# Attention decode, forward and backward: the spared DMA engine's rows dealt to other pairs of engines in each of five stores

## The chip, the cores and the metric

The kernel runs on 1 core of one Trainium2 chip. The metric is the device time of that core in microseconds (us), lower is better. Before the change it was 1276.73 us, the median of 3 runs (1276.36 to 1278.41).

## What is computed

64 heads (2 batches of 32), one query row each, 8192 keys and values of 128 numbers, all in bf16. The reference gives the attention output and the gradients of q, k and v:

```python
def _fwd_reference(q, k, v):
    scale = q.shape[-1] ** -0.5
    scores = jnp.einsum("bhqd,bhkd->bhqk", q, k) * scale
    p = _softmax(scores, axis=-1)
    return jnp.einsum("bhqk,bhkd->bhqd", p, v)

_out, _vjp = jax.vjp(_f, q, k, v)      # outputs: _out and the three gradients
_grads = _vjp(grad_out)
```

With one query row, the gradients of v and k are outer products: dV is the softmax weights times the row of grad_out, dK is the score gradient times the row of q. So 2 x 64 tensors of 2 MB are read (K and V of each head) and 2 x 64 of 2 MB are written (dK and dV). Nothing else that crosses to memory is large.

## The kernel before, in words

**Tiles.** K and V of one head each lie in a tile of 128 partitions (`kt`, `vt`), 64 tokens of 128 numbers on a partition, which is one contiguous row of 16 KB in memory. There are 5 such pairs of tiles (`UNITS`). SyncE's queue (SP) loads them with one transfer of 128 rows each (`load`, issued from L106).

**One head's work.** TensorE turns the tile in 64 steps (L115), ScalarE copies the results out of PSUM (L122, two of them in a head by VectorE, L120), TensorE forms the scores and the products with grad_out (L131), small steps form the softmax (L148 to L244), and TensorE sums the weighted rows (L256). VectorE then writes the outer products into the very tiles from which K and V were read (`outer`, L288: dV over `vt`, dK over `kt`), and the tiles are stored. The main loop interleaves the front half of head h with the back half of head h-1, in an order written out by hand.

**Stores.** `store(h, w, ...)` (w = 0 for dV, 1 for dK) issues one transfer of 128 rows of 16 KB from ScalarE's queue (L348). As ScalarE's instructions run in order, the issue of a store also stands ahead of the copies of L122 behind it. The last head is stored in halves.

**Five stores by pieces.** For one store in 26 (`RARE`; 2h + w = 12, 38, 64, 90, 116, always a dV) `store_by_fifteen` takes over and issues from GpSimd's queue (POOL). It sends the 128 rows in 24 transfers: for each r of 0 to 3 transfers of 11, 4, 2, 3, 8 and 4 rows (L316). The 16 DMA engines that move everything are called 0 to 15 here. A transfer of n rows from this queue puts its rows on n neighbouring engines, the next one goes on where it ended, and a tiny transfer `turn(n)` (L302: n rows of 2 x 4 bytes from q into the scratch tile `spare`) moves the starting place on by n without moving data that matters. The transfers of 4 rows are sent in pieces of 16 KB and not of 8 KB; they start at engine 0 and leave the starting place where it is. The packets of the trace bear this reading out: four engines have forty 16 KB packets of this queue each, one engine has no data packet of it. In this way the rows are laid so that the fifth engine (number 4) gets none: engine 0 to 3 and 5 to 15 get 8 rows each in a store, which is 120, and the 8 rows that engine 4 would have had (partitions 16 to 19 and 48 to 51) go in four transfers of 2 rows to four pairs of neighbouring engines. Those four transfers are `fifth(r)` before the change.

**What orders these transfers.** GpSimd runs its instructions in order. Eight semaphores are used in turn for the transfers of its queue, so each transfer waits for the landing of the one eight before it. After a store by pieces the tile it left is next loaded ten heads later (V of head 16 is the first load that waits for GpSimd's transfers), because the pool gives out tiles in the order in which they come free.

Of the kernel before, what the change touches and what calls it, by code (L numbers as in the profile page):

```python
# [16 lines left out]
QG = 4  # L17
OG = 4
RARE = 26
UNITS = 5  # L20


@with_exitstack
def kernel(
# [41 lines left out]

    kvp = ctx.enter_context(tc.tile_pool(name="kv", bufs=UNITS))
    evp = ctx.enter_context(tc.tile_pool(name="ev", bufs=5))
# [29 lines left out]
    def load(h):  # L98
        x = heads[h]
        x.ev = {}  # L100
        x.kv = [
            kvp.tile([P, NT, D], BF16, name="kt", tag="kt"),
            kvp.tile([P, NT, D], BF16, name="vt", tag="vt"),
        ]
        for dst, src in zip(x.kv, (k_v, v_v)):
            nc.sync.dma_start(out=dst[:], in_=src[h])  # L106
# [108 lines left out]
    def weights_v(h):  # L215
        x = heads[h]
        x.rl, x.rls = rl_all[:, 0, h : h + 1], rl_all[:, 1, h : h + 1]
        to_weights(0, x.E)
        nc.vector.reciprocal(out=x.rl, in_=x.lsum)
        x.w2 = [doubled("P2", x.E, x.rl)]  # L220
        nc.vector.tensor_scalar(
            out=x.rls, in0=x.rl, scalar1=scale, scalar2=None, op0=ALU.mult
        )
# [73 lines left out]
    def turn(n):  # L297

        i = 4 * len(turns)
        turns.append(n)  # L300
        two = lambda t: t.rearrange("p (a b) -> p a b", a=2)
        nc.gpsimd.dma_start(  # L302
            out=two(spare[0:n, :])[:, :, i : i + 2], in_=two(q_rows[0:n, :])[:, :, 0:2]
        )

    def store_by_fifteen(h, w):

        dst, src = (dv_v, dk_v)[w][h], heads[h].kv[1 - w]

        def rows(lo, n, step=4, size=8192):
            own = slice(lo, lo + step * (n - 1) + 1, step)
            nc.gpsimd.dma_start(out=dst[own], in_=src[own], max_dma_last_dim=size)  # L316

        def fifth(r):
            rows(16 + r, 2, step=32)

        for r in range(4):

            if r == 1:
                fifth(r)
                turn(14)
            rows(52 + r, 11)
            rows(r, 4, size=16384)
            if r == 0:
                fifth(r)
                turn(3)  # L330
            elif r == 3:
                turn(10)
                fifth(r)
                turn(9)
            else:
                turn(5)
            rows(20 + r, 3)
            if r == 2:
                fifth(r)
                turn(14)  # L340
            rows(96 + r, 8)
            rows(32 + r, 4, size=16384)
            turn(5)

    def store(h, w, a=0, b=NT):
        if (2 * h + w) % RARE == RARE // 2 - 1:
            return store_by_fifteen(h, w)
        nc.scalar.dma_start(out=(dv_v, dk_v)[w][h][:, a:b, :], in_=heads[h].kv[1 - w][:, a:b, :])  # L348
# [28 lines left out]
    with tc.manual_schedule():  # L377
        for h in range(min(UNITS, BH)):
            load(h)
        for h in range(BH + 1):  # L380
# [4 lines left out]
            for j in range(NS):  # L385
# [45 lines left out]
                if y and j == 7:  # L431
                    weights_v(h)
                    if x and UNITS <= h + 3 < BH:
                        load(h + 3)
                if y and j == 4 and h % QG == 0:
                    spread_rows(h // QG)
        for w, dst in enumerate((o_rows, dq_rows)):
            tps = ps_tp.tile([BH, P], BF16, name="tps", tag="tp")
            nc.tensor.transpose(tps[:], colsT[:, w, :], ident_bf[:])  # L439
            rows = const.tile([BH, D], BF16, name=f"rows{w}")  # L440
# [33 lines left out]
```

## Time and profile before

| what | value |
|---|---|
| median of 3 runs | 1276.73 us |
| the profiled execution's own time | 1276.51 us |
| its span (first to last instruction) | 1274.4 us |
| mean granted TensorE clock | 0.933 |
| busy: TensorE, VectorE, ScalarE, GpSimd | 1060.1, 892.3, 961.0, 104.5 us |
| memory read, written | 268.47 MB, 268.47 MB |
| mean rate over the span | 421 GB/s |
| store by pieces: first issue, last issue, the first one | 138.6 us, 221.7 us |
| store by pieces: first issue, last issue, the fifth one | 1164.1 us, 1244.8 us |

The span counts from the first instruction of the program; the 2.1 us between the span and the execution's time lie around it. "DMA" in the profile's strip is the mean busy share of the 16 DMA engines in each of 40 equal slices, in tenths. The lines of the DMA queues give packets, MB, and the time of their packets as a share of 16 engines' span: q1 is SP's loads, q10 ScalarE's stores, q0 GpSimd's transfers, q8 and q14 the queues that the profile calls "instruction". A packet is here one 16 KB row (or an 8 KB half of one in most pieces of GpSimd's), or one of the few bytes that report an engine's share of a transfer as landed.

### The profile page before, as it was taken

Reading aid. Unit: us, or ns where it says so; the run is one execution under the profiler, and the core shown is the slowest. Engines: PE = TensorE matmul, PEld = TensorE weight load, DVE = VectorE, ACT = ScalarE, POOL = GpSimd, SP = SyncE. Lnnn points to the kernel's source line nnn. Section 1 sums busy time; section 2 is a strip of 40 time slices with the busy share of each in tenths; the row PEclk is TensorE's granted clock in tenths of the full one; section 3 lists DMA queues with packets and bytes.
Section 4 is the critical chain, followed back from the end, with each engine's and each line's share of the span. In section 5 each row is a group of like instructions: output and inputs, shape, how many; then the busy total and the mean of one; then the engine's idle time right before and its main releaser. Section 6 shows DMA issues by size and latency. Waiting matters only on the chain. (4 is left out here: it accounts for less than half of the span.)

```text
span 1274.4 us, 31597 instructions
## 1 busy us (share of the span) xinstructions
PE 1060.1 (83%) x13444; PEld 708.9 (56%) x13444; DVE 892.3 (70%) x1576; ACT 961.0 (75%) x1107; POOL 104.5 (8%) x189
## 2 busy tenths in 40 slices
PE   5999889849998798399996984999969849999694
PEld 4666566526665565266664652666546526666462
DVE  1888858728887487288884863888856738888486
ACT  5888778739887687289875873988848838888583
POOL 1000211000002110000021200000212000001220
PEclk9999989969999799699997996999989979999797
DMA  9999999999999999999999999999999999999998
GB/s 394 419 429 426 428 426 427 426 431 429 427 428 426 425 426 427 426 422 427 428 426 423 424 426 425 422 426 429 425 418 427 428 428 415 429 427 428 424 425 345
DMA packets 43837, 539.00 MB, mean 423 GB/s; under 512 B 10192, under 2 KB 10192, under 8 KB 10192
## 3 DMA queue, kind: packets, MB, share of 16 engines
q1 hardware_dynamic: 18432, 268.44, 49.7%
q10 hardware_dynamic: 18320, 258.02, 47.7%
q0 software_dynamic: 6944, 10.51, 2.2%
q8 instruction: 105, 1.72, 0.5%
q14 instruction: 36, 0.29, 0.1%
HBM read 268.47 MB, written 268.47 MB: 421 GB/s over the span
## 5 line engine op out<-in xcount | busy, mean ns | idle before, releaser
L122 ACT CAST ev<-tp 128x1024 bf16<-128x1024 f32 x960 | 933.3, 1017 | 290.0 <-PE tp L115 141.2
L115 PE MATMUL tp<-ident_bf,vt 128*128 128x128 bf16 x4096 | 328.9, 226 | 132.3 <-ACT ev L122 117.2
L115 PEld LDWEIGHTS <-vt 128*128 128x128 bf16 x4096 | 266.7, 102 | 210.3 <-issue 185.0
L115 PE MATMUL tp<-ident_bf,kt 128*128 128x128 bf16 x4096 | 318.7, 221 | 8.8 <-DMA kt<-in_k_dram 7.2
L115 PEld LDWEIGHTS <-kt 128*128 128x128 bf16 x4096 | 238.9, 98 | 135.7 <-issue 124.5
L288 DVE TENSOR_TENSOR vt<-qd,P 128x2048 bf16<-128x2048 bf16 x256 | 306.6, 1219 | 0.2 <-DVE rawsb L142 0.2
L288 DVE TENSOR_TENSOR kt<-qd,dS 128x2048 bf16<-128x2048 bf16 x256 | 306.1, 1217 | 0.0
L131 PE MATMUL raw<-ev,qz 128*4 128x512 bf16 x2048 | 202.3, 384 | 0.3 <-ACT ev L122 0.3
L142 DVE COPY rawsb<-raw 128x512 f32<-128x512 f32 x128 | 88.6, 692 | 132.9 <-PE raw L131 130.5
L316 POOL DMA_DIRECT2D out_dram<-vt x120 | 67.0, 560 | 1018.5 <-DVE vt L288 822.4
L174 DVE TENSOR_REDUCE mp<-turned 128x1 f32<-128x64 f32 x64 | 14.1, 221 | 131.0 <-PE turned L148 130.2
L256 PE MATMUL acc<-vt,wz 128*32 128x512 bf16 x1024 | 102.1, 389 | 0.0
L256 PE MATMUL acc<-kt,wz 128*32 128x512 bf16 x1024 | 100.9, 387 | 0.9 <-DVE wz L203 0.9
L148 PE MATMUL turned<-ident_f,rawsb 128*128 128x128 f32 x512 | 87.4, 296 | 11.6 <-DVE rawsb L142 9.8
L120 DVE CAST ev<-tp 128x1024 bf16<-128x1024 f32 x64 | 78.4, 1225 | 16.7 <-PE tp L115 16.7
L131 PEld LDWEIGHTS <-qz 128*4 128x4 bf16 x2048 | 46.5, 81 | 55.3 <-issue 3.9
L148 PEld LDWEIGHTS turned<-ident_f,rawsb 128*128 128x128 f32 x512 | 57.1, 147 | 29.5 <-DVE rawsb L142 29.3
L256 PEld LDWEIGHTS <-wz 128*32 128x32 bf16 x2048 | 52.4, 93 | 29.2 <-DVE wz L203 1.6
L180 DVE TENSOR_REDUCE gm<-misc 1x1 f32<-1x128 f32 x64 | 17.8, 279 | 45.2 <-PE misc L178 45.2
L200 PEld LDWEIGHTS misc<-ld,ones_f 128*128 128x128 f32 x256 | 38.4, 189 | 15.3 <-DVE ld L227 15.3
L200 PE MATMUL misc<-ld,ones_f 128*128 128x1 f32 x256 | 45.9, 248 | 0.7 <-DVE ld L227 0.6
L302 POOL DMA_DIRECT2D spare<-in_q_dram x57 | 34.2, 600 | 123.0 <-DMA out_dram<-vt 107.8
(45 smaller groups left out, 332.7 us busy)
## 6 DMA issues: line engine op xcount, KB each, us to landing
kt<-in_k_dram SPq DMA_DIRECT2D x64, 2048.0 KB, 21.4
vt<-in_v_dram SPq DMA_DIRECT2D x64, 2048.0 KB, 30.6
out_dram<-kt ACTq DMA_DIRECT2D x63, 2048.0 KB, 24.9
out_dram<-vt ACTq DMA_DIRECT2D x58, 2048.0 KB, 22.5
out_dram<-vt POOLq DMA_DIRECT2D x20, 176.0 KB, 22.6
out_dram<-vt POOLq DMA_DIRECT2D x40, 64.0 KB, 22.8
out_dram<-vt POOLq DMA_DIRECT2D x20, 128.0 KB, 22.5
out_dram<-vt ACTq DMA_DIRECT2D x2, 1024.0 KB, 8.6
```

Source lines behind the costliest of these rows:

```text
L115: nc.tensor.matmul(tp[:, i, :], lhsT=x.kv[w][:, n, :], rhs=ident_bf[:], start=True, stop=True)
L120: nc.vector.tensor_copy(out=ev[:], in_=tp[:])
L122: nc.scalar.copy(out=ev[:], in_=tp[:])
L131: nc.tensor.matmul(raw[32 * k : 32 * k + 4, :], lhsT=qz[w][:, at : at + 4], rhs=evs[k // 2][:, 4 * (k % 2) : 4 * (k % 2) + 4, :].rearrange ...
L142: nc.vector.tensor_copy(out=x.raw[:], in_=raw[:])
L148: nc.tensor.transpose(out[:, i], x.raw[:, i * P : (i + 1) * P], ident_f[:])
L180: nc.vector.reduce_max(out=x.gm[:], in_=mT, axis=AX.X)
L200: nc.tensor.matmul(x.lsum, lhsT=ones_f[:], rhs=x.ld[:, w : w + 1], start=True, stop=True)
L256: nc.tensor.matmul(acc[32 * g : 32 * g + 32, :], lhsT=wz[w][:, n // 4, at : at + 32], rhs=rows[:, n : n + 4, :].rearrange("p n d -> p (n d)"),
L288: nc.vector.tensor_tensor(out=x.kv[1 - w][:, n : n + CH, :].rearrange("p n (d t) -> p n d t", t=2), in0=row.unsqueeze(1).to_broadcast([P, ...
L302: nc.gpsimd.dma_start(out=two(spare[0:n, :])[:, :, i : i + 2], in_=two(q_rows[0:n, :])[:, :, 0:2])
L316: nc.gpsimd.dma_start(out=dst[own], in_=src[own], max_dma_last_dim=size)
```

## The change

It rewrites the body of `store_by_fifteen`. The starting engines of the four transfers of 2 rows come from a table, one row of it for each of the five stores, and such a transfer always stands behind the first transfer of 4 rows. A `turn(e)` leads to engine e, and a `turn((3 - e) % 16)` leads on, so that 5 places in all are passed, as before.

```diff
+EXTRA = ((0, 5, 8, 10), (2, 6, 12, 14), (0, 7, 10, 13), (2, 5, 9, 15), (1, 7, 11, 13))
...
-        def fifth(r):
-            rows(16 + r, 2, step=32)
-
-        for r in range(4):
-
-            if r == 1:
-                fifth(r)
-                turn(14)
+        for r, e in enumerate(EXTRA[(2 * h + w) // RARE]):
             rows(52 + r, 11)
             rows(r, 4, size=16384)
-            if r == 0:
-                fifth(r)
-                turn(3)
-            elif r == 3:
-                turn(10)
-                fifth(r)
-                turn(9)
-            else:
-                turn(5)
+            if e:
+                turn(e)
+            rows(16 + r, 2, step=32)
+            turn((3 - e) % 16)
             rows(20 + r, 3)
-            if r == 2:
-                fifth(r)
-                turn(14)
             rows(96 + r, 8)
             rows(32 + r, 4, size=16384)
             turn(5)
```

Before, the pairs begin at engines 0, 5, 8 and 10 in every store. After, they begin at the four engines of the store's row of the table. The transfers of rows are the same 24 in each store; the tiny ones are 57 in the program before and 60 after. Nothing is changed on another engine.

## Prediction

> **What bounds the kernel now.** I read the page's strip of slices first, then its DMA queues, then the table by stretches and the timeline around the last stall, then the single DMA packets that the trace holds.
>
> ```profile
> DMA  9999999999999999999999999999999999999998
> GB/s 394 419 429 426 428 426 427 426 431 429 427 428 426 425 426 427 426 422 427 428 426 423 424 426 425 422 426 429 425 418 427 428 428 415 429 427 428 424 425 345
> ...
> q1 hardware_dynamic: 18432, 268.44, 49.7%
> q10 hardware_dynamic: 18320, 258.02, 47.7%
> q0 software_dynamic: 6944, 10.51, 2.2%
> q8 instruction: 105, 1.72, 0.5%
> ```
>
> The 16 DMA engines are busy from end to end, and no other engine is (TensorE 83%). The queue lines give prices. q1 took 49.7% of 16 x 1274.4 us for 16384 rows of 16 KB, 0.62 us a row. q8, the instruction queue, has 105 packets for 0.5%, 0.97 us each. GpSimd's stores by pieces are the 10.51 MB of q0.
>
> The stretches around the last stall, and the timeline there, show how the DMA engines set the end:
>
> ```profile
> 1180.00:1185.00 5.00, 2.57 (x36) 1.34 (x34) 3.35 (x5) 1.35 (x2) 0.55 (x1) 1.00 1.01 423
> 1185.00:1190.00 5.00, 0.00 (x0) 0.00 (x0) 0.99 (x1) 0.00 (x0) 1.17 (x2) 0.59 1.01 428
> 1190.00:1195.00 5.00, 1.60 (x11) 1.06 (x11) 0.00 (x0) 2.48 (x3) 1.11 (x2) 0.50 1.00 410
> 1195.00:1200.00 5.00, 5.00 (x43) 3.91 (x41) 1.79 (x5) 3.62 (x6) 1.17 (x2) 0.55 1.01 426
> ```
>
> ```profile
> 1190.72 0.33 SPq L106 DMA_DIRECT2D kt<-in_k_dram  x1
> ...
> 1191.90 0.34 ACTq L348 DMA_DIRECT2D out_dram<-vt  x1
> 1192.34 1.93 ACT L122 CAST ev<-tp 128x1024 bf16<-128x1024 f32 x2 [10.99 <-issue]
> ```
>
> TensorE (first pair of columns) stands still from 1185 to 1190 while the DMA share stays at 1.01. ScalarE's next copies waited 11 us behind the issue of a store, which itself waited for an earlier transfer to land; SP's load was let go 1.2 us before. From 1191.9 us to the end TensorE and VectorE hardly wait, so the end is this landing plus about 82.5 us of work. A transfer lands when the slowest of 16 engines has done its part. So the question is which DMA engines are slowest, and by how much.
>
> That I took from the single packets. On a DMA engine a packet starts 3 to 4 ns before the one ahead of it ends, which strings the packets into sixteen chains; the sequence of GpSimd's packets on a chain tells its number (neighbours with equal duties stay undecided). What differs between chains, beyond equal loads and stores:
> - **Instruction packets.** 104 of the 105 fall on eight chains, 13 each: 5, 6, 10, 11, one of 8 and 9, three of 12 to 15. Such a packet takes 0.88 to 1.07 us, median 0.95, and the row behind it about 1.00 in place of 0.61. So 13 cost 13 x (0.95 + 0.39 - 0.02 overlap) = 17.2 us.
> - **Engine 4.** Its stores have a median of 0.645 us a row where others have 0.611, its loads some 0.012 more. Without the few rows over 0.70 us, which are waits, this is 968 x 0.029 + 1024 x 0.012 = 40 us; the 40 rows that it is spared give back 40 x 0.61 = 24.4. It stands at +15.7.
> - **The rows of engine 4** go to 0, 1, 5, 6, 8, 9, 10, 11 now: 5 rows each, 3.05 us.
>
> Engines with both, 5, 6, 10, 11 and one of 8 and 9, stand at +20.2 us; instruction packets alone +17.2; engine 4 +15.7; the rest 0 to +3. The gaps agree: between 40 and 1190 us, waits (rows over 0.70 us, less those behind instruction packets, plus idle gaps) come to 1 to 5 us, 2 in the mean, on the engines with instruction packets and 8 to 15 us on those without, engine 4 aside.
>
> **The change part by part.**
> - *Removed:* the five times repeated pairs, 5 rows on each of eight engines.
> - *Added:* the table's pairs. Counted out, engines 0 to 15 get 3, 3, 3, 2, none, 2, 3, 3, 3, 2, 3, 3, 2, 3, 3, 2 rows. The count is worked out from the code: before, the quarters pass 2 + 3, 2 + 14 + 5, 5 + 2 + 14 and 10 + 2 + 9 places, all 5 modulo 16; after, e + 2 + (3 - e) is 5 too, so all other rows stay where they were and engine 4 stays empty.
> - *Worth of it.* Engines 10, 11 and 6 go from 20.2 to 17.2 + 3 x 0.61 = 19.0, engine 5 to 18.4; 12 to 14 rise from 17.2 to 18.4 or 19.0. If the single slowest engine sets the time, the gain is 2 x 0.61 = 1.2 us. If the eight take turns at being last (their instruction packets come in rotation, one about every 10 us), their mean counts: five of eight had 5 rows, mean 3.1; after, 2.6; gain 0.3 us. At 1191.9 us four of five stores are through, and the count is 4 against 3 at most: 0.6 us. I take 0.8, between the ends.
> - *Three more tiny transfers* (57 to 60), in the second, fourth and fifth store. Each is 0.61 us of GpSimd, 8% busy. The issues of a store stand 83 us / 35 = 2.4 us apart, because each waits for the one eight before it, so these stores end 2.4 us later. What hides it: the tile of the first store by pieces is loaded next at 274.7 us, its last piece issued at 221.7 landed by about 244, 30 us ahead; in the fifth store the last issue is at 1244.8, and SP's closing wait for `spare` was over by 1257.5 (1274.4 less the 16.9 it then waited for the last rows). Without that cover each costs 2.4 us, at most 7. On the DMA engines a tiny packet is 5 ns from start to start: nothing.
> - *Moved:* in the second quarter the pair goes from ahead of the 11 rows to behind them, in the third from behind the 3 rows to ahead; the longest move is 4 transfers, 10 us inside an 80 us store. Nothing but the tile's next load, above, waits for one piece. POOL's queue holds nothing else; SP's and ScalarE's instructions stay as they are.
>
> Sum: 1276.51 (the profiled run, 0.2 under the median of 1276.73) less 0.8 = **1275.7 us**. The bounds of the unknown part are 0 and 1.2 of gain.
>
> One rule speaks against the change. The row first: chain 7 waits 9.1 us in rows over 0.70 us of its loads, and the slow chain in this trace is 4, with 0.645 us a store. The Trainium skill ("DMA: Bandwidth & Descriptors", section "Latency and other measured facts") says that engines 7 and 15 are usually slower than the rest, and calls its reason a guess; the trace does not agree for 7, and cannot tell 15 from 12 to 14. By that rule the sum would be the third rival's. The same page (section "Why a DMA increments its semaphore by 16 and not by 1") says that a transfer from GpSimd's queue takes consecutive engines from a round-robin cursor; the chains here agree (forty 16 KB packets on each of four, none of data on engine 4).
>
> **The rivals.**
> 1. *No gain, engine 4 is the bound* (chance 0.17): its 15.7 is worked out from a threshold of 0.70 us; if its long rows are no waits, it is 15.7 + 5.3 = 21.0, above 20.2. The change leaves it alone: 1276.5. Against it: it shows 0.7 us of idle gaps.
> 2. *Slower, engines 12 to 14 are the bound* (0.13): they have the instruction packets and no extra rows today, and now get 2 or 3 each. This decides if they are the last when the store at 1191.9 waits. In favour: at the 85th load two of them stood 11.7 and 13.0 us behind the earliest engine, as far as 10 and 11 (12.2, 12.8). Price 1.2 to 1.8 us: 1278.3; with the runs' own spread of 2 us it may pass 1279.3.
> 3. *The rule on engines 7 and 15* (0.05): if either were the last, 3 or 2 rows more cost it 1.8 or 1.2 us: 1278.5. Against it for 7: its waits.
> 4. *The places are not as I count* (0.04): if a moved start put the rest of a store off by one, engine 4 would get up to 8 rows in a store, 4.9 us; five stores cost up to 24 us, 1281 to 1300. Against it: the sums modulo 16 above.
> 5. *More than counted* (0.13): if a store's extra rows meet an instruction packet on one engine just where a load is waited for, and this now happens less, 0.61 + 1.32 us can drop out once or twice: 1273 to 1274.5.
>
> **How the numbers follow.** The forecast has 0.48. A measurement of this kernel can tell about 0.2% (2.6 us) from no change: faster means under 1274.2, slower over 1279.3. The forecast and the first rival lie within, and most of the second and third. Faster comes from rival 5, with a little of the forecast's spread: 0.15. Slower from rival 4, half of 2 with the spread of runs, some of 3: 0.12. Same: 0.73. The range reaches to rival 5's middle and past the second and third, 1273.0 to 1279.0.
>
> **What would show it.** Right: the chains of 10, 11, 5 and 6 have 42 or 43 rows of GpSimd's stores in place of 45, engine 4 still none, 60 tiny transfers, DMA strip unchanged, last stall again near 1185 to 1192 us within 1.5 us. Wrong: a chain 4 with rows of GpSimd's, a slice with a DMA share under 9 around a store by pieces, a load of V let go later because of GpSimd's transfers, or a last stall that moved by over 2.5 us.

## The result, and the profile after

The changed kernel takes 1299.59 us (median of 5 runs, 1297.65 to 1300.66), the kernel before 1276.86 (5 runs). The ratio is 1.0172, with a 95% interval of 1.0158 to 1.0185: 22.7 us slower. The forecast, 1275.7 in a range of 1273.0 to 1279.0, was wrong. The profiled execution took 1297.65 us, its span is 1295.9, the granted clock 0.931 (0.933 before).

From the page of after, the strip, the queues and the median times from issue to landing (last column, us):

```profile
DMA  9999999999999999999999999999999999999996
GB/s 394 419 428 428 428 426 425 428 431 427 427 427 427 427 425 430 413 420 429 427 422 409 414 427 400 415 425 428 427 396 422 423 378 404 427 428 427 398 415 267
...
q1 hardware_dynamic: 18432, 268.44, 49.4%
q10 hardware_dynamic: 18320, 258.02, 47.0%
q0 software_dynamic: 7040, 10.51, 2.2%
q8 instruction: 105, 1.72, 0.5%
...
kt<-in_k_dram SPq DMA_DIRECT2D x64, 2048.0 KB, 23.7
vt<-in_v_dram SPq DMA_DIRECT2D x64, 2048.0 KB, 32.3
out_dram<-kt ACTq DMA_DIRECT2D x63, 2048.0 KB, 26.2
```

The same three lines of the page of before:

```profile
kt<-in_k_dram SPq DMA_DIRECT2D x64, 2048.0 KB, 21.4
vt<-in_v_dram SPq DMA_DIRECT2D x64, 2048.0 KB, 30.6
out_dram<-kt ACTq DMA_DIRECT2D x63, 2048.0 KB, 24.9
```

The bytes are the same and no queue does more work. The three tiny transfers more are the 96 packets more of q0. What is new are holes in the rate: before, no slice but the first and the last is under 415 GB/s; here the lowest of them stand at 409, 400, 396, 378, 404 and 398, all from the middle of the run on. A load of K lands in 23.7 us, in 21.4 before. The tenths of the DMA line hide this: a mean of 0.95 is a 9 too.

SP's timeline at the last long stall, and the table by stretches there (the pairs of columns are TensorE's matmuls and weight loads, VectorE, ScalarE, GpSimd; then clock, DMA share, GB/s):

```profile
1207.26 0.33 SPq L108 DMA_DIRECT2D kt<-in_k_dram  x1
1207.68 0.38 SPq L108 DMA_DIRECT2D vt<-in_v_dram  x1
1218.45 0.33 SPq L108 DMA_DIRECT2D kt<-in_k_dram  x1
1229.56 0.33 SPq L108 DMA_DIRECT2D vt<-in_v_dram  x1
```

```profile
1202.00:1204.00 2.00, 0.00 (x0) 0.00 (x0) 1.65 (x2) 0.00 (x0) 0.00 (x0) 1.00 0.99 422
1204.00:1206.00 2.00, 0.00 (x0) 0.00 (x0) 0.00 (x0) 0.00 (x0) 0.56 (x1) 0.78 0.99 418
1206.00:1208.00 2.00, 0.00 (x0) 0.00 (x0) 0.00 (x0) 0.00 (x0) 0.57 (x1) 0.50 0.77 316
1208.00:1210.00 2.00, 0.00 (x0) 0.00 (x0) 0.00 (x0) 0.00 (x0) 0.55 (x1) 0.50 0.83 266
```

The load of K that SP let go at 1190.7 before is let go at 1207.3. Before, the DMA engines kept a share of 1.00 to 1.01 while TensorE stood still. Here the share falls to 0.77 and 0.83 and the rate to 266: in the mean three to four of the 16 stand idle. The packets show what is waited for. From 1207.3 to 1214.1 us the rows of ScalarE's stores run one at a time, seven in all, six of them at 615 to 632 ns where 611 is usual: a single engine has fallen behind the others with its part. Of the stores' packets that report a part as landed, the last one before ScalarE goes on comes at 1209.4 us, between two of these rows; ScalarE issues its next store at 1210.3. The forecast had named this as a sign against it: a last stall moved by over 2.5 us.

When the time was lost shows in the landing of the loads (counted from 0; the time of landing is that of before, the difference is after less before):

| load | lands at about (us) | later by (us) |
|---|---|---|
| 56 | 533 | 0.2 |
| 64 | 615 | 2.7 |
| 88 | 853 | 9.5 |
| 112 | 1090 | 13.9 |
| 120 | 1171 | 17.1 |
| 127 | 1242 | 22.0 |

Nothing is lost up to 533 us. The first store by pieces (139 to 222 us) is as good as before; the loss begins behind the second (389 to 473 us).

**Which engine.** The three `turn(1)` of the table (second store, fourth and fifth, each in the first quarter) stand out in the packets. The 57 tiny transfers of before show 16 packets of 8 bytes each, 912. After has 60 of them and again 912: the three `turn(1)` show packets of 4 bytes alone, 32 each, two on every chain (4912 before, 5008 after). Worked out from the code with a `turn(1)` that moves the starting place by nothing, the rows of the five stores on engines 0 to 15 are:

```
       0   1   2   3   4   5   6   7   8   9  10  11  12  13  14  15
1st    9   9   8   8   0   9   9   8   9   9   9   9   8   8   8   8
2nd    8   8   9   9   7   9   9   8   8   8   8   9   9   9   9   1
3rd    9   8   8   8   8   8   9   9   8   9   9   8   9   9   8   1
4th    8   9   9  16   9   8   8   9   9   8   8   8   8   9   2   0
5th    8   8  15  16   9   9   8   8   9   9   9   9   8   1   1   1
sum   42  42  49  57  33  43  43  42  43  43  43  43  42  36  28  11
```

All sixteen chains of the trace agree with this, without one difference over the 71 transfers of the first two stores; with one or two places for a `turn(1)` there are up to 7 and 11 differences. The slow chain, with the 0.645 us rows, has no row in the first store and 7 in the second. So each `turn(1)` put all that follows one engine lower, and engine 4 got 33 rows.

### The profile page after: what moved, and what is told of

Same layout as the page of the kernel before. It is cut to its first block, busy times and chain, and to the rows that moved or that the text cites. A ratio compares the mean times of both kernels' runs of the same rounds, so it can differ in the third digit from the quotient of the medians.

```text
span 1295.9 us, 31600 instructions
## 1 busy us (share of the span) xinstructions
PE 1064.1 (82%) x13444; PEld 712.0 (55%) x13444; DVE 892.2 (69%) x1576; ACT 961.5 (74%) x1107; POOL 105.8 (8%) x192
## 5 line engine op out<-in xcount | busy, mean ns | idle before, releaser
L117 PE MATMUL tp<-ident_bf,kt 128*128 128x128 bf16 x4096 | 322.5, 223 | 18.0 <-DMA kt<-in_k_dram 16.7
L117 PEld LDWEIGHTS <-kt 128*128 128x128 bf16 x4096 | 241.8, 99 | 147.2 <-issue 125.5
## 6 DMA issues: line engine op xcount, KB each, us to landing
kt<-in_k_dram SPq DMA_DIRECT2D x64, 2048.0 KB, 23.7
```

Source lines behind the costliest of these rows:

```text
L117: nc.tensor.matmul(tp[:, i, :], lhsT=x.kv[w][:, n, :], rhs=ident_bf[:], start=True, stop=True)
```

## The experiments

The theory (A in the expectations): a `turn(1)` doesn't move the starting place, and the time comes from the rows that engine 4 then gets. Its rivals: the new pairs themselves cost the time; or it is that rows are sent by other engines than their own, whichever these are. A row's own engine is the one that the first store gives it, with partitions 16 to 19 and 48 to 51 belonging to engine 4. Each expectation names the rivals that it is set against. Ratios are to the kernel before, run beside it on the same chip, with 95% intervals; differences in us are those of the two medians, which differ by up to 1.4 us from what the ratio gives.

**The table with the starts as meant.** After, with a 9 and an 8 (17, one around the ring) where it has a 1:

```diff
+        def on(n):
+            for m in (9, 8) if n == 1 else (n,) if n else ():
+                turn(m)
...
-            if e:
-                turn(e)
+            on(e)
             rows(16 + r, 2, step=32)
-            turn((3 - e) % 16)
+            on((3 - e) % 16)
```

> The changed kernel, with each of its three turn(1) replaced by turn(9) and turn(8), which pass 17 places, the same place modulo 16; the table of pairs stays. Theory A (turn(1) moves the starting place by 0, so that from the second store on engine 4 gets rows): the places are as the table means them, 1275.7 us, between 1275.3 and 1276.9. Theory B (the other pairs themselves cost the time): 1297 to 1300, as the changed kernel. Three more tiny transfers cost nothing in either.

Measured: 1277.41 us, ratio 1.0001 (0.9993 to 1.001). The whole 22.7 us is gone with the three `turn(1)`, and no transfer of rows was changed for it. The pairs as the cause fall, and the holes of the strip are gone (from the page of this run):

```profile
GB/s 393 419 430 427 428 426 424 427 429 429 427 428 427 427 425 428 430 425 427 428 426 427 426 426 422 424 427 428 427 416 420 427 421 416 427 429 426 416 423 339
```

The table itself is worth nothing that these runs can tell; a gain of 0.8 us lies at the interval's edge.

**A turn(1) in the kernel before.** One extra move of 1 + 15 = 16 places, ahead of the second store:

```diff
+        if 2 * h + w == 38:
+            turn(1)
+            turn(15)
```

> The kernel before, with turn(1) and turn(15) put ahead of the second store by pieces; its pairs stay. Together they pass 16 places, which is none, if a turn(1) moves by 1. Theory A (turn(1) moves by 0): all later rows lie one engine lower, engine 4 gets 9 rows in each of four stores, 36 in all, 36 x 0.61 = 22 us more for it: from +15.7 to +37.7 where +20.2 was the bound, so at least 17 us slower, 1294, up to 1301. Theory B: two tiny transfers more, 1276.9.

Measured: 1305.28 us, 1.0209 (1.0195 to 1.0223). Two transfers of a few bytes cost 28 us, so a `turn(1)` doesn't pass one place, and this without any table. It is more than the 1301 that the theory allowed for the 36 rows that engine 4 gets here; that excess is taken up below. The strip has the same holes, and they come with each later store:

```profile
GB/s 394 421 428 430 424 428 423 427 429 427 428 428 418 411 415 420 372 429 426 430 423 409 418 429 393 423 427 429 427 397 417 422 381 394 428 427 428 393 398 267
```

**Is it the one row, or the shape?** `turn(n)` writes n x 2 x 2 values through a pattern of three levels; with n = 1 the first falls away and two are left. The pieces of 16 KB, which never moved the start, have two levels as well. So: 15 rows, in two levels.

```diff
+        if 2 * h + w == 38:
+            i = 4 * len(turns)
+            turns.append(15)
+            nc.gpsimd.dma_start(out=spare[0:15, i : i + 2], in_=q_rows[0:15, 0:2])
```

> The kernel before, with one tiny transfer of 15 rows ahead of the second store, written as one piece of 4 bytes a row and not as two (a pattern of two levels, as the rows of 16 KB are, where all turns have three). Theory A1 (patterns of two levels do not move the starting place, whatever their number of rows; turn(1) is one of them since its single row leaves two levels): no change, 1276.9. Theory A2 (it is the single row that does not move): 15 rows move by 15, all later rows lie one engine lower, 1294 to 1301.

Measured: 1276.7 us, 0.9992 (0.9976 to 1.0008). Had it moved the start by 15, all later stores would lie one engine lower, as in the run above. Its packets also look like those of a `turn(1)`: 32 of 4 bytes (4944 in place of 4912), none of 8. So it is the shape: on this queue the transfers of two levels that these kernels send don't move the starting place (or move it by 16, once around, which comes to the same), with 15 rows as with one. The Trainium skill ("DMA: Bandwidth & Descriptors", section "Why a DMA increments its semaphore by 16 and not by 1") says that the slowest dimension above 1 decides on how many engines a transfer uses, which for a 1 x 2 x 2 would pass two places, and names an exception of this queue: some direct copies are dealt over all 16. The runs agree with the exception for the patterns of two levels, and not with two places for a `turn(1)`.

**Displaced rows without engine 4.** Before, with one place more from the second store on. Engine 4 still gets none, engine 0 gets 73 in all, and in four stores the rows of engines 5 to 15 are sent by the next one up:

```diff
+        if 2 * h + w == 38:
+            turn(9)
+            turn(8)
```

> The kernel before, with turn(9) and turn(8) ahead of the second store by pieces: 17 places, so all later rows that follow the starting place lie one engine higher. Engine 4 still gets none, engine 5 gets 9 instead of 45, engine 0 gets 73 instead of 45. Theory A (what counts is that engine 4 gets rows): engine 0, which has no instruction packets, stands at 33 x 0.61 = +20.1, as far as the slowest now (+20.2): 1277 to 1280. Theory C (any displacement costs, because rows lie on other engines than the loads and stores of ScalarE's queue have them): as the run with turn(1) and turn(15), 1300 to 1305.

Measured: 1279.35 us, 1.0017 (1.0008 to 1.0026): 2.3 us, within what theory A gave; theory C falls. Engine 0's 33 rows more are 33 x 0.61 = 20.1 us, level with the forecast's bound of 20.2, so some of this may be theirs. Rows displaced upwards by one, with engine 4 spared, cost no more than this here. What displaced rows cost while engine 4 lags is another matter, taken up below.

**One store one engine lower.** Engine 4 gets 9 rows in the second store, and none later:

```diff
+        if 2 * h + w == 38:
+            turn(15)
+        if 2 * h + w == 64:
+            turn(9)
+            turn(8)
```

> The kernel before, with turn(15) ahead of the second store by pieces and turn(9) and turn(8) ahead of the third, so that one store alone lies one engine lower: engine 4 gets 9 rows in all. Theory A with a threshold (the time is that of the slowest engine, and engine 4 has 4 to 5 us in hand): +15.7 + 9 x 0.61 = +21.2 against +20.2, 1 us slower, 1278 (1276.9 to 1280). Rival (each such store costs the same): a quarter of 28 us, 1284.

Measured: 1281.28 us, 1.0034 (1.0023 to 1.0045): 4.3 us, between what the theory and its rival gave. By the forecast's terms (below) 9 rows on engine 4 are worth 1 of it.

**No store by pieces at all.** All stores go from ScalarE's queue; engine 4 has all of its 40 rows, in their place:

```diff
     def store(h, w, a=0, b=NT):
-        if (2 * h + w) % RARE == RARE // 2 - 1:
-            return store_by_fifteen(h, w)
```

> The kernel before with all 128 stores issued from ScalarE's queue, none by pieces: engine 4 has all its 40 rows, and nothing is displaced. Theory A: engine 4 stands at +40 where the bound was +20.2, 20 us slower, 1297 (1294 to 1300). If the measured cost of rows on engine 4 is higher than 0.61 us each, as 22.7 us for 33 rows suggests: up to 1304. Theory C (displacement): no slower than before, 1274 to 1277.

Measured: 1295.25 us, 1.0139 (1.0126 to 1.0152): 18.2 us, the whole worth of sparing engine 4. After is slower than that: it spares 7 rows and loses 4.3 us more.

**Engine 4's rows in place, the rest by pieces.** From the second store on, the pieces of 16 KB take a fifth row, that of engine 4's own partition, and there are no pairs:

```diff
+        if 2 * h + w > 12:
+            for r in range(4):
+                rows(52 + r, 11)
+                rows(r, 5, size=16384)
+                turn(5)
+                rows(20 + r, 3)
+                rows(96 + r, 8)
+                rows(32 + r, 5, size=16384)
+                for n in (14, 7) if r else (5,):
+                    turn(n)
+            return
```

> The kernel before, with the second to fifth store by pieces sent without sparing engine 4 and without displacing a row: the transfers of 4 rows become 5 rows in pieces of 16 KB, which start at engine 0 and so give engine 4 its own 8 rows; no pairs; as many transfers (35) as before. Engine 4 has 32 rows, about the 33 that the changed kernel gives it, all other engines 40. Theory A in its plain form (0.61 us a row, whatever the place): engine 4 at +15.7 + 32 x 0.61 = +35.2 against +20.2, 15 us slower, 1292. Theory A with a charge for displaced rows (the 7 us by which 33 displaced rows cost more): 1290 to 1293 here, against 1299.6 of the changed kernel. Theory D (the loss beyond 15 us comes with stores by pieces themselves while engine 4 lags, wherever the rows lie): 1298 to 1302.

Measured: 1295.64 us, 1.0148 (1.0134 to 1.0162): 19.1 us for 32 rows, above the 1290 to 1293 and below the 1298 to 1302 that were expected. The strips of this kernel and of the one without stores by pieces, in this order, show two ways to lose about the same time, 19.1 and 18.2 us:

```profile
GB/s 395 416 429 428 424 426 427 428 430 429 427 427 427 427 427 416 419 429 428 428 426 409 427 412 404 427 429 428 426 381 428 430 376 421 427 428 428 392 412 269
```

```profile
GB/s 394 420 428 427 427 428 430 428 427 429 427 431 427 428 428 427 422 425 424 421 424 423 425 420 419 416 418 422 415 418 420 414 426 416 416 420 417 413 370 254
```

With stores by pieces the rate falls in single slices (404, 381, 376, 392), without them a little everywhere (413 to 426 from 800 us on, but for the last two).

**A simpler placement: the eight rows on engines 0 to 3.** After, with engine 4's rows as two transfers of four neighbouring partitions in pieces of 16 KB ahead of a store, and `turn(5)` alone:

```diff
+        for lo in (16, 48):
+            rows(lo, 4, step=1, size=16384)
```

> The kernel before, with engine 4's 8 rows of a store sent in two transfers of 4 rows in pieces of 16 KB, which start at engine 0 and move nothing: engines 0 to 3 get 50 rows in all, 5 to 15 get 40, engine 4 none; no turn around them. If the eight engines with the instruction packets set the time, their +20.2 falls to +17.2 and 0 to 3 stand at +6.1: up to 3 us faster, 1273.8 (1273.5 to 1276). If engine 4 is the bound: 1276.9. If such transfers did not start at engine 0: slower, up to 1300.

Measured: 1301.84 us, 1.0191 (1.0176 to 1.0206). A miss of 28 us, with the rows placed as meant (the chains show engine 4 empty). The stretches around the start of the first store (137.7 us), first of this run, then of the kernel before:

```profile
140.00:150.00 10.00, 9.30 (x119) 6.55 (x116) 7.36 (x16) 8.92 (x12) 2.82 (x5) 1.00 1.03 388
150.00:160.00 10.00, 6.13 (x85) 3.54 (x86) 7.89 (x11) 4.38 (x5) 1.71 (x3) 1.00 0.98 415
```

```profile
140.00:150.00 10.00, 9.30 (x122) 6.55 (x120) 7.32 (x14) 8.99 (x12) 4.30 (x8) 1.00 1.00 425
150.00:160.00 10.00, 7.07 (x98) 4.15 (x96) 8.84 (x14) 6.06 (x7) 1.72 (x3) 1.00 1.01 429
```

In the first 10 us the engines are no less busy than before and move less (388 GB/s in place of 425): their packets take longer. The eight rows of these transfers took 0.84 to 3.84 us in this store where a row of 16 KB from partitions four apart takes 0.61; over the kernel the 200 pieces of 16 KB lie 101.7 us above that in all, against 0.5 us for the 160 of before. q0 rose to 2.6% with the same bytes.

**The pairs away from the engines with instruction packets.** After with `on()` of the first experiment and

```diff
+EXTRA = ((0, 2, 7, 15),) * 5
```

> The changed kernel with the places of 1 made by turn(9) and turn(8), and with pairs that begin at 0, 2, 7 and 15 in every store, engines without instruction packets but 8 or 9 at most: 5, 6 and 9 to 14 get 40 rows, engine 0 gets 50, 1, 2, 3, 7, 8 and 15 get 45, engine 4 none. If the engines with instruction packets set the time: +20.2 falls to +17.2, 1273.9, or 1275 if they take turns. If engine 4 is the bound: 1276.9, no change.

Measured: 1274.54 us, 0.9983 (0.9974 to 0.9991): 2.5 us faster than before (by the interval 1.1 to 3.3), and so faster than both kernels. The strip, of an execution that took 1276.51 us, has no hole:

```profile
DMA  9999999999999999999999999999999999999998
GB/s 394 418 426 430 427 425 425 427 429 429 427 429 427 427 426 428 430 426 427 429 424 422 426 425 425 425 427 429 427 421 426 426 426 419 427 429 427 424 426 334
```

**One step further.** The same, and in each store the first quarter's transfers of 3 and 8 rows go in pieces of 16 KB to engines 0 to 3, which takes rows off the eight:

```diff
+            if r == 0:
+                rows(20 + r, 3, size=16384)
+                rows(96 + r, 4, size=16384)
+                rows(112 + r, 4, size=16384)
+                rows(32 + r, 4, size=16384)
+                continue
```

> The run with pairs at 0, 2, 7 and 15, with the first quarter of each store changed: its 3 and its 8 rows go in pieces of 16 KB to engines 0 to 3, so that the engines with instruction packets have 35 rows and not 40 in the five stores, engine 0 has 65, engine 3 about 55. If the engines with instruction packets are still the bound there: 3 us less, +14.2, but engine 4 at +15.7 and engine 0 at +15 stand in the way: 1273 (1272.5 to 1274.5). If engine 4 is the bound already: as that run, 1274.5. If rows away from their own engine's partitions cost, as 40 packets of 0.8 to 5.2 us did where four neighbouring partitions were sent at once: slower, 1277 to 1285.

Measured: 1279.41 us, 1.0029 (1.0015 to 1.0043): 2.9 us slower than before, where the step before was 2.5 us faster. In the profiled execution ScalarE's stores took 125 us in all above 0.61 a row; in those of the kernel before and of the step before they took 80. That rows sent by engines far from their own hold up others fits this, but no run isolates it. The pieces of 16 KB themselves, 55 more than before and from partitions four apart, were not slow: the 215 lie 4.7 us above 0.61 in all. So in the run with four neighbouring partitions it was not being sent by another engine alone that made the rows slow.

## Why the prediction was wrong, by its steps

**The step that failed.** "the quarters pass ... all 5 modulo 16; after, e + 2 + (3 - e) is 5 too, so all other rows stay where they were and engine 4 stays empty." The sum is right on paper and wrong on the chip: three of its terms are a `turn(1)`, and that passes 0 places, shown by the kernel before with one such transfer (1.0209) and by after without them (1.0001). The same sets right what stands ahead of the prediction, that a `turn(n)` moves the starting place on by n: it holds for the other n that these kernels use (1.0001 with those alone), not for 1. The trace of before held no `turn(1)`, so the price of one could not be read there. It held a warning, which the front part even tells: the pieces of 16 KB don't move the start. I took that for a property of those pieces and didn't ask which form of transfer it belongs to.

**Rival 4** ("The places are not as I count", chance 0.04, 1281 to 1300) is what happened: "engine 4 would get up to 8 rows in a store, 4.9 us; five stores cost up to 24 us". Engine 4 got 7, 8, 9 and 9 (33 rows by the count that fits the chains), and the cost was 22.7 us. The chance was too small, since the one argument against it, the sums, took for granted what the rival denies.

**The price of a row on engine 4** held in its kind, not in its size. By the forecast's own terms, engine 4 stands at 15.7 + 0.61 x rows against a bound of 20.2:

| kernel | rows on engine 4 | by the terms (us) | measured (us) |
|---|---|---|---|
| one store lower | 9 | 1.0 | 4.3 |
| rows in place, by pieces | 32 | 15.0 | 19.1 |
| after | 33 | 15.6 | 22.7 |
| turn(1), turn(15) | 36 | 17.5 | 28.1 |
| no store by pieces | 40 | 19.9 | 18.2 |

Without stores by pieces the terms are right within 2 us. With them, 3 to 4 us come on top where the rows are few or in place, 7 to 11 where all later stores lie on other engines. In the kernel with `turn(1)` and `turn(15)`, engine 4's 18 pieces of 8 KB in the second store took about 440 ns in the mean, where 309 is usual. That a lagging engine 4 and displaced stores hold each other up would fit this, but it isn't shown; which wait carries the 7 to 11 us stays open.

**The engines with instruction packets as the bound** is borne out. Moving the 5 extra rows away from them gave 2.5 us; by the terms the slowest falls from 20.2 to 17.2 (3.0 us), and the mean of the eight by 5 x 3.05 / 8 = 1.9. **The gain of 0.8 us** by spreading these rows isn't confirmed: 1.0001, with 0.8 us at the edge of the interval.

**The three tiny transfers** cost nothing that shows, as forecast: the kernel with the starts as meant has 63 of them, six more than before, and a ratio of 1.0001; the fastest has 62.

**Rivals 1, 2, 3 and 5** had no chance to show in after. Of the rule on engines 7 and 15, rival 3: the fastest kernel gives both five rows more than before, so neither set the time of before. With the starts as meant the kernel is 0.2 us slower than the one before, by the interval 0.9 faster to 1.3 slower. That is nearest to rival 1's no change; the forecast's gain of 0.8 and the lower end of rival 2's 1.2 to 1.8 lie just inside. But rival 1's reason, that engine 4 alone is the bound, doesn't agree with the gain of the fastest kernel, which leaves engine 4 as it is.

## What to carry to other kernels

A count that rests on hidden state, such as a starting place that each transfer moves on, is only as good as its rarest form: list the shapes that the change issues, and for each one that the trace of before doesn't show, price what happens if it moves the state by another amount. Here one transfer of 8 bytes, with a leading dimension of 1, cost up to 28 us. And before work is spread evenly over engines, see which of them carry other duties: moving rows off those gave 2.5 us, the even spread nothing that could be told.

## What the runs showed of the hardware

- On GpSimd's queue, the transfers of these kernels whose pattern has two levels leave the starting place where it is (15 rows: 0.9992; 1 row: 28 us of consequences), those of three levels move it on by their rows (the first two stores of after, place by place).
- Rows of 16 KB from four neighbouring partitions, sent by four engines at once, took 0.84 to 3.84 us in one store, from partitions four apart 0.61, also where other engines than their own sent them (55 of 215 pieces; all 215 lie 4.7 us above that).
- Sparing one slow engine (0.645 us a row where others have 0.611) 40 of its 1024 rows of stores is worth 18.2 us of 1295.
